# Exchanging halves of the rows by DMA in place of halves of the weights by VectorE

## The chip, the cores and the metric

One NeuronCore of a Trainium2 chip runs the kernel. The metric is the device time of one execution in microseconds (us), the median of several executions. Three executions of the kernel before took 1431.30, 1432.51 and 1433.72 us: the median is 1432.51 us.

## The reference

The input x has 8 sequences of 3584 tokens with 192 channels, 28672 rows in all.

1. A causal convolution over 7 tokens, whose 8 heads of 24 channels have softmaxed taps of their own, gives the rows.
2. Each row is normalised and multiplied with 8 normalised expert embeddings; the largest logit picks the expert, and the softmax of the logits at that place is the gate.
3. The row goes through the picked expert alone: `out = gate * (relu(row @ w1[e]) @ w2[e])`, with w1[e] 192 x 1024 and w2[e] 1024 x 192.

All is float32. The kernel carries nearly that precision through float16 matrices: each operand is a high half plus a low half, and a product is three float16 products (high x high, high x low, low x high).

## The kernel before

The rows are cut into 16 chunks of 1792 rows. For each chunk the kernel runs `mix` (convolution on TensorE, copies and squares on ScalarE and VectorE), then `route` (split into halves, transposition, logits, expert and position of each row), and then writes the chunk's rows to a table in DRAM (`rows_d`) that has one region for each expert, by 16 indirect DMAs from GpSimd. Each row of the table has the 192 high halves, then the low halves in the order of channels 128 to 191 and 0 to 127, then the token's number and its gate.

After chunks 2, 3, 4, 6, 9 and 12 and at the end (`PICK`, `hand_out`), blocks of 1024, 512 or 256 rows of one expert that are complete are appended to a list; blocks of 128 come at the very end. A block of 1024 is two entries of 512. Each entry is called a sub-block here; there are 92 sub-blocks in 88 blocks, numbered from 0. In the profile a sub-block has forty matmuls of line 750 and one transposing load of line 709, so that both can be counted off.

For a sub-block `expert` does this:

- `fetch` loads and transposes its rows from the table to SBUF by a transposing DMA (line 709, tile `e_xT`, three buffers), and its token numbers and gates by a small DMA (line 712). At the start of sub-block n, `fetch` is called for sub-block n+2. Where the list ends earlier, the call comes later. `e_xT` has three planes of 128 partitions: plane 0 the high halves of channels 0 to 127, plane 1 the high halves of channels 128 to 191 (partitions 0 to 63) and their low halves (64 to 127), plane 2 the low halves of channels 0 to 127.
- `copy_w1` and `copy_w2`, once for each block: VectorE copies the expert's image from `res` (all eight experts, in SBUF) to `slot`, since matmuls read at fixed addresses. The image has, side by side, W1's high part, W1's low part, one plane with the high (partitions 0 to 63) and low part (64 to 127) of W1's rows 128 to 191, and W2. `copy_w1` copies the first three (line 688, 3072 columns) and makes a fourth plane, the third with its halves exchanged, by two copies of 64 partitions (lines 690 and 691). It is called when the layer 1 of the sub-block before is written down, `copy_w2` (line 694) inside layer 1.
- Layer 1: each of eight groups of 128 hidden units takes five matmuls (line 750): plane 0 and plane 2 with W1's high part, plane 0 with W1's low part, plane 1 with the third plane of weights, plane 1 with the fourth. The last two give high x high plus low x low, and high x low plus low x high, of channels 128 to 191. The groups lie in PSUM tiles of 512 columns, for which a ring of five is shared with layer 2. ScalarE writes the rectified high half to `hid` (line 754), VectorE the low half (line 756).
- Layer 2: 24 matmuls for each 128 rows (line 773), scaled by the gate on ScalarE (line 778) and written to `out` by an indirect DMA from GpSimd (line 780).

SyncE's instructions, and with them all its DMAs, stand in the order in which the program writes them: the fetches, the transpositions of the routed rows (`turn`, line 580) and the loads of x (line 358) share this one queue, and one that waits holds all behind it. On the other engines a planner orders the instructions by a simulated time line, before the kernel runs; `under` and `behind` pin an instruction behind another of the same engine. `expert` is a generator: between its steps `run` writes down so many steps of `mix` and `route` as `steer` allots by fixed costs.

Before all that, `prep_load` and `prep_weights` bring each expert's weights to a staging area (in `hid`, `slot` or the end of `res`, in turn), measure their scale and split them into the image.

Of the kernel before, what the change touches and what calls it, by code (L numbers as in the profile page):

```python
# [37 lines left out]
RES = WS + 2  # L38
S2 = 4 * F
PAD = 128  # L40
# [15 lines left out]
LAND_X, LAND_T = 9.0, 4.5  # L56
TURN, FETCH, PIECE = 5.1, 2.1, 1.4
RANK_L, RANK_P = 2.0, 1.5
# [17 lines left out]
class _Moe:  # L76
    def __init__(self, ctx, tc, x, weight, emb, tau, w1, w2, out):
# [34 lines left out]
        self.weights_in, self.later = False, []  # L112
        self.subs, self.ready, self.at, self.copied = [], 0, 0, 0

# [151 lines left out]
    def prep_load(self, e):  # L266
        nc = self.nc


        st = (self.hid[:], self.slot[:], self.res[:, (E - 2) * RES:])[e % 3].bitcast(F32)[:, 0:2 * F + NFC * D]  # L270
        w1, w2 = self.w1[e], self.w2[e]
        nc.sync.dma_start(out=st[:, 0:F], in_=w1[0:128, :])
        nc.sync.dma_start(out=st[0:64, F:2 * F], in_=w1[128:192, :])
        nc.sync.dma_start(
            out=st[:, 2 * F:].rearrange("p (c d) -> p c d", d=D),
            in_=w2.rearrange("(c p) d -> p c d", p=128))
        return st

    def prep_weights(self, e, st):
# [3 lines left out]

        sr = st.bitcast(BF16).rearrange("p (n k) -> p n k", k=2)[:, :, 1]
        acc = self.sp.tile([128, 2], F32, tag="w_acc", name="w_acc")
        for k, cols in enumerate(
                ([(128, i) for i in range(NFC)] + [(64, i) for i in range(NFC, 2 * NFC)],
                 [(128, i) for i in range(2 * NFC, 2 * NFC + NFC * D // 128)])):
            if k and e >= BEHIND:

                i = nc.scalar.activation(
                    out=img[:, W2:W2 + NFC * D], in_=st[:, 2 * F:], func=AF.Square,
                    accum_out=acc[:, k:k + 1]).ins
# [4 lines left out]
            for n, (rows, i) in enumerate(cols):  # L298
                v = sr[0:rows, i * 128:(i + 1) * 128]
# [17 lines left out]
        b = img[:, W2:WS].rearrange("p (c d) -> p c d", d=2 * D)  # L317
        s_b = st[:, 2 * F:].rearrange("p (c d) -> p c d", d=D)
        hi = [nc.scalar.activation(out=o, in_=i, func=AF.Copy, scale=m).ins
# [357 lines left out]
    def copy_w1(self, at):  # L677
# [9 lines left out]
        v = self.res[:, bass.ds(self.we, W2)]  # L687
        nc.vector.tensor_copy(out=self.slot[:, 0:W2], in_=v)  # L688
        v = self.res[:, bass.ds(self.we + 2 * F, F)]
        nc.vector.tensor_copy(out=self.slot[0:64, W2:S2], in_=v[64:128, :])  # L690
        nc.vector.tensor_copy(out=self.slot[64:128, W2:S2], in_=v[0:64, :])  # L691

    def copy_w2(self):
        self.nc.vector.tensor_copy(  # L694
            out=self.slot[:, S2:], in_=self.res[:, bass.ds(self.we + W2, RES - W2)])
# [28 lines left out]


    def slack(self, T):
        pe = 5 * T / 2400
        return max(0, pe - (120 + T) / 960), max(0, pe - (172 + T) / 1200)


    def expert(self):
        nc, tc = self.nc, self.tc
        while self.ready < min(self.at + 3, len(self.subs)):
            self.fetch()
        u, xT, mt, T = self.subs[self.at][3:]
# [4 lines left out]
        w2 = self.slot[:, S2:S2 + WS - W2].rearrange("p (c d) -> p c d", d=2 * D)  # L740
        hh, hl = (self.hid[:, i * NFC * T:(i + 1) * NFC * T].rearrange(
# [3 lines left out]
        for b in range(0, NFC, m):  # L745
            ps = self.ps("h", [128, m, T], F32, "h_ps")
            for c in range(m):
                for i, (o, k) in enumerate(
                        ((0, 0), (0, 2), (F, 0), (2 * F, 1), (3 * F, 1))):
                    self.mm = nc.tensor.matmul(  # L750
                        out=ps[:, c, :], lhsT=w1(o, b + c), rhs=xT[:, k, :],
                        start=(i == 0), stop=(i == 4)).ins
# [13 lines left out]
            out=g[:, 0:nj], in0=mt[:, :, 1].bitcast(F32),  # L766
            scalar1=self.slot[:, S2 + WS - W2:S2 + WS - W2 + 2].bitcast(F32), scalar2=None, op0=ALU.mult)
        for a in range(nj):
# [193 lines left out]
```

## Time and profile before

| | |
|---|---|
| median of three executions | 1432.51 us |
| the profiled execution | 1439.81 us |
| its span, first to last instruction | 1438.1 us |
| TensorE busy in the span | 1199.9 us (83%) |
| VectorE busy | 862.3 us (60%) |
| ScalarE busy | 573.1 us (40%) |
| GpSimd busy | 547.5 us (38%) |
| mean granted TensorE clock | 0.913 of full speed |

The engines are PE (TensorE matmul), PEld (its weight loads, which overlap PE), DVE (VectorE), ACT (ScalarE), POOL (GpSimd) and SP (SyncE); a q behind the name is the engine's sequencer, which waits and issues DMAs. L750 is line 750 of the kernel before. A timeline row gives the start, the length, the engine, the line, what is written and what is read, the count of instructions merged in the row, and in brackets the idle time before it and what ended it.

### The profile page before, as it was taken

Reading aid. Unit: us, or ns where it says so; the run is one execution under the profiler, and the core shown is the slowest. Engines: PE = TensorE matmul, PEld = TensorE weight load, DVE = VectorE, ACT = ScalarE, POOL = GpSimd, SP = SyncE. Lnnn points to the kernel's source line nnn. Section 1 sums busy time; section 2 is a strip of 40 time slices with the busy share of each in tenths; the row PEclk is TensorE's granted clock in tenths of the full one; section 3 lists DMA queues with packets and bytes.
Section 4 is the critical chain, followed back from the end, with each engine's and each line's share of the span. In section 5 each row is a group of like instructions: output and inputs, shape, how many; then the busy total and the mean of one; then the engine's idle time right before and its main releaser. Section 6 shows DMA issues by size and latency. Waiting matters only on the chain. (4 is left out here: it accounts for less than half of the span.)

```text
span 1438.1 us, 28996 instructions
## 1 busy us (share of the span) xinstructions
PE 1199.9 (83%) x10560; PEld 918.6 (64%) x10560; DVE 862.3 (60%) x2208; ACT 573.1 (40%) x1345; POOL 547.5 (38%) x566
## 2 busy tenths in 40 slices
PE   5531956978878988899888989868999999999997
PEld 3421645856766756776554656636777676788797
DVE  3935666765866647677665666544454656467465
ACT  4734624344425425355335433222333333333332
POOL 0054042344454355445564455454222222222232
PEclk9655878988999989899999999979999999999999
DMA  8325262544445353573654452422121212012120
GB/s 249 116 71 177 55 148 53 114 111 113 101 116 119 83 137 82 123 135 79 142 142 96 104 118 73 93 68 65 44 48 40 46 41 57 28 42 60 32 49 22
DMA packets 273952, 129.11 MB, mean 90 GB/s; under 512 B 215774, under 2 KB 264285, under 8 KB 273808
## 3 DMA queue, kind: packets, MB, share of 16 engines
q1 hardware_dynamic: 250000, 80.39, 25.9%
q0 software_dynamic: 23808, 46.87, 11.0%
q8 instruction: 82, 1.34, 0.4%
q14 instruction: 62, 0.51, 0.1%
HBM read 38.35 MB, written 47.53 MB: 60 GB/s over the span
## 5 line engine op out<-in xcount | busy, mean ns | idle before, releaser
L750 PE MATMUL h_ps<-e_xT,slot 128*128 128x256 f16 (+2 forms) x3680 | 567.2, 307 | 48.1 <-issue 22.8
L773 PE MATMUL o_ps<-slot,hid 128*128 128x192 f16 x5544 | 523.2, 252 | 59.1 <-issue 18.7
L773 PEld LDWEIGHTS <-hid 128*128 128x128 f16 x5544 | 474.4, 100 | 107.1 <-issue 49.6
L780 POOL DMA_INDIRECT out_dram<-y,e_mt x231 | 261.5, 1132 | 586.3 <-ACT y L778 546.1
L750 PEld LDWEIGHTS <-slot 128*128 128x128 f16 x3680 | 330.0, 100 | 240.5 <-issue 76.3
L756 DVE SCALAR_TENSOR_TENSOR hid<-h_ps,hid 128x512 f16<-128x512 f32 x462 | 313.2, 687 | 203.4 <-ACT hid L754 178.1
L754 ACT ACTIVATE hid<-h_ps 128x512 f16<-128x512 f32 x462 | 267.7, 598 | 359.2 <-PE h_ps L750 236.2
L584 POOL DMA_INDIRECT rows_d<-rows,di x256 | 263.6, 1030 | 212.3 <-ACT hid L754 72.0
L778 ACT ACTIVATE y<-o_ps,g 128x192 f32<-128x192 f32 x231 | 91.6, 418 | 301.1 <-PE o_ps L773 165.7
L694 DVE COPY slot<-res 128x3074 f16 x88 | 85.8, 975 | 202.7 <-PE h_ps L750 150.9
L399 PE MATMUL conv_ps<-xt,band 128*112 128x384 f32 x256 | 108.7, 528 | 34.4 <-DMA xt<-in_dram 16.4
L404 ACT COPY xt<-conv_ps 112x384 f32<-112x384 f32 x128 | 60.3, 481 | 79.4 <-PE conv_ps L399 60.0
L688 DVE COPY slot<-res 128x3072 f16 x88 | 84.8, 963 | 9.2 <-remote 7.3
L485 PEld LDWEIGHTS <-xT 128*112 128x112 f16 x768 | 59.7, 145 | 37.2 <-DMA xT<-rows 17.0
L485 PE MATMUL lg_ps<-ma,xT 128*112 128x16 f16 x512 | 60.2, 201 | 20.4 <-DMA xT<-rows 12.0
L399 PEld LDWEIGHTS conv_ps<-xt,band 128*112 128x112 f32 x256 | 41.7, 189 | 52.0 <-issue 20.5
L411 ACT ACTIVATE sq<-xt 112x192 f32<-112x192 f32 x192 | 67.9, 357 | 3.9 <-DVE sq L414 2.8
L448 ACT CAST rows<-xt 112x768 f16<-112x768 f32 x64 | 49.9, 832 | 35.9 <-POOL rows L440 31.6
L446 DVE TENSOR_TENSOR xt<-xt,x_p_s 112x768 f32<-112x768 f32 x64 | 58.3, 948 | 0.0
L450 DVE TENSOR_TENSOR rows<-xt,rows 112x512 f16<-112x512 f32 x64 | 43.8, 684 | 15.7 <-ACT rows L448 15.6
L485 PE MATMUL lg_ps<-mb,xT 128*112 128x16 f16 x256 | 47.4, 204 | 1.5 <-ACT xT L481 1.5
L414 DVE SCALAR_TENSOR_TENSOR sq<-xt 112x192 f32<-112x192 f32 x64 | 22.6, 355 | 36.1 <-ACT sq L411 33.7
(165 smaller groups left out, 547.6 us busy)
## 6 DMA issues: line engine op xcount, KB each, us to landing
xt<-in_dram SPq DMA_DIRECT2D x39, 384.0 KB
xt<-in_dram SPq DMA_DIRECT2D x3, 1440.0 KB
rows_d<-rows,di POOLq DMA_INDIRECT x256
out_dram<-y,e_mt POOLq DMA_INDIRECT x231
xT<-rows SPq DMA_TRANSPOSE x224
xt<-in_dram SPq DMA_DIRECT2D x2, 1536.0 KB
hid<-in_dram SPq DMA_DIRECT2D x3, 768.0 KB
slot<-in_dram SPq DMA_DIRECT2D x3, 768.0 KB
```

The lines of the kernel that those rows point to most:

```text
L399: i = nc.tensor.matmul(out=ps, lhsT=self.band[:, h, :], rhs=xt[:, :, h * G:(h + 1) * G], start=True, stop=True).ins
L411: nc.scalar.activation(out=sq, in_=xc[:, t, :], func=AF.Square, accum_out=n2[:, t:t + 1])
L485: i = nc.tensor.matmul(out=lg[:, g * GX + a, :], lhsT=xT[:, a, k, :], rhs=self.mb if k == 1 else self.ma, start=(k == 0), stop=(k == 2)).ins
L584: i = self.nc.gpsimd.indirect_dma_start(out=self.rows_d[:, :], out_offset=bass.IndirectOffsetOnAxis(ap=idx, axis=0), in_=src, in_offset=No ...
L688: nc.vector.tensor_copy(out=self.slot[:, 0:W2], in_=v)
L694: self.nc.vector.tensor_copy(out=self.slot[:, S2:], in_=self.res[:, bass.ds(self.we + W2, RES - W2)])
L750: self.mm = nc.tensor.matmul(out=ps[:, c, :], lhsT=w1(o, b + c), rhs=xT[:, k, :], start=(i == 0), stop=(i == 4)).ins
L754: self.step = nc.scalar.activation(out=hh[:, b:b + m, :], in_=ps, func=AF.Relu).ins
L756: self.low = nc.vector.scalar_tensor_tensor(out=hl[:, b:b + m, :], in0=ps, scalar=0.0, in1=hh[:, b:b + m, :], op0=ALU.max, op1=ALU.subtrac ...
L773: self.mm = nc.tensor.matmul(out=o, lhsT=h[:, c, q], rhs=w2[:, c, k:k + D], start=(c + i == 0), stop=(c == NFC - 1 and i == 2)).ins
L778: self.step = nc.scalar.activation(out=y, in_=o, func=AF.Copy, scale=g[:, a:a + 1]).ins
L780: i = nc.gpsimd.indirect_dma_start(out=self.out[:, :], out_offset=bass.IndirectOffsetOnAxis(ap=mt[:, a, 0:1], axis=0), in_=y, in_offset=No ...
```

## The change

1. `copy_w1` no longer makes the fourth plane of weights; lines 690 and 691 go, and `slot` is 1024 columns shorter.
2. For each sub-block a new step `flip` makes a fourth plane of rows, `xf`: plane 1 with its halves exchanged, by two DMAs inside SBUF of 64 partitions each, from SyncE's queue, in two buffers. `flip` for sub-block n is written down ahead of `fetch` for sub-block n+1, and where that has not come by then, at the start of sub-block n.
3. The fifth matmul of a group takes the third plane of weights with `xf`; the others are as they were.
4. The one copy of W1 that stays is pinned behind the last low half written down (`under`).
5. The staging areas are dealt out anew, since `slot` is too short for one: W1 of experts 0, 3 and 6 goes to `slot` and their W2 to a stretch of `res` that the image of expert 7 takes later; experts 1, 4 and 7 use `hid`; 2 and 5 use the end of `res` as before.

```diff
-TURN, FETCH, PIECE = 5.1, 2.1, 1.4
+TURN, FETCH, PIECE, FLIP = 5.1, 2.1, 1.4, 0.9
...
+        self.fp = pool("flip", 2)
...
-        self.slot = self.cp.tile([128, S2 + RES - W2], F16, name="slot")
+        self.slot = self.cp.tile([128, RES], F16, name="slot")
...
-        st = (self.hid[:], self.slot[:], self.res[:, (E - 2) * RES:])[e % 3].bitcast(F32)[:, 0:2 * F + NFC * D]
+        tail = self.res[:, (E - 2) * RES:]
+        n1, n2 = 4 * F, 2 * NFC * D
+        s1, s2 = ((self.slot[:, 0:n1], tail[:, n1 + n2:n1 + 2 * n2]),
+                  (self.hid[:, 0:n1], self.hid[:, n1:n1 + n2]),
+                  (tail[:, 0:n1], tail[:, n1:n1 + n2]))[e % 3]
+        s1, s2 = s1.bitcast(F32), s2.bitcast(F32)
...
         v = self.res[:, bass.ds(self.we, W2)]
-        nc.vector.tensor_copy(out=self.slot[:, 0:W2], in_=v)
-        v = self.res[:, bass.ds(self.we + 2 * F, F)]
-        nc.vector.tensor_copy(out=self.slot[0:64, W2:S2], in_=v[64:128, :])
-        nc.vector.tensor_copy(out=self.slot[64:128, W2:S2], in_=v[0:64, :])
+        self.under(nc.vector.tensor_copy(out=self.slot[:, 0:W2], in_=v).ins)
...
     def fetch(self):
         nc, tc = self.nc, self.tc
+        if self.ready > self.flips:
+            self.flip()
...
+    def flip(self):
+        nc = self.nc
+        xT, mt, T = self.subs[self.flips][4:7]
+        xf = self.fp.tile([128, 512], F16, tag="xf", name="e_xf")[:, 0:T]
+        nc.sync.dma_start(out=xf[0:64, :], in_=xT[64:128, 1, :])
+        nc.sync.dma_start(out=xf[64:128, :], in_=xT[0:64, 1, :])
+        self.queue(FLIP)
+        self.subs[self.flips] = self.subs[self.flips][:4] + (xT, mt, T, xf)
+        self.flips += 1
...
         while self.ready < min(self.at + 3, len(self.subs)):
             self.fetch()
-        u, xT, mt, T = self.subs[self.at][3:]
+        if self.flips == self.at:
+            self.flip()
+        u, xT, mt, T, xf = self.subs[self.at][3:]
         self.copy_w1(self.at)
         self.at += 1
...
+        xk = [xT[:, 0, :], xT[:, 1, :], xT[:, 2, :], xf]
...
-                        ((0, 0), (0, 2), (F, 0), (2 * F, 1), (3 * F, 1))):
+                        ((0, 0), (0, 2), (F, 0), (2 * F, 1), (2 * F, 3))):
                     self.mm = nc.tensor.matmul(
-                        out=ps[:, c, :], lhsT=w1(o, b + c), rhs=xT[:, k, :],
+                        out=ps[:, c, :], lhsT=w1(o, b + c), rhs=xk[k],
```

## Rows read from the trace of the kernel before

**Rows 1.** stretch, length; busy us of PE, PEld, DVE, ACT, POOL; clock, DMA
```profile
...
160.00:950.00 790.00, 669.61 (x5581) 500.96 (x5580) 504.59 (x1450) 326.06 (x848) 373.19 (x381) 0.92 0.46 107
...
1100.00:1400.00 300.00, 288.20 (x2962) 234.87 (x2961) 176.44 (x291) 103.08 (x203) 76.84 (x68) 1.00 0.20 45
...
```

**Rows 2.** waits of TensorE from 160 to 950: total us, times, longest
```profile
...
PE h_ps L750 <- DMA e_xT<-rows_d: 10.0, 1, 10.0
PE o_ps L773 <- DVE hid L756: 8.8, 17, 2.0
...
PE o_ps L773 <- DVE slot L694: 3.7, 3, 1.8
...
```

**Rows 3.** waits of TensorE from 1100 to 1400, same columns
```profile
...
PE o_ps L773 <- DVE slot L694: 5.8, 13, 0.9
PE o_ps L773 <- DVE hid L756: 4.9, 11, 0.5
...
```

**Rows 4.** VectorE copies, groups by form: busy us, mean ns, idle before
```profile
...
L688 DVE COPY slot<-res 128x3072 f16 x88 | 84.8, 963 | 9.2 <-remote 7.3 <-PE h_ps L750 0.8 <-PE conv_ps L399 0.7
...
L691 DVE COPY slot<-res 64x1024 f16 x88 | 39.2, 446 | 1.5
L690 DVE COPY slot<-res 64x1024 f16 x88 | 37.4, 424 | 2.2
...
```

**Rows 5.** VectorE timeline around 609: start us, us, what
```profile
...
608.67 0.96 DVE L688 COPY slot<-res 128x3072 f16 x1
...
610.55 0.69 DVE L756 SCALAR_TENSOR_TENSOR hid<-h_ps,hid 128x512 f16<-128x512 f32 x1
...
```

**Rows 6.** ScalarE and VectorE timeline, preparation of weights
```profile
...
118.49 1.48 ACT L291 ACTIVATE res<-slot 128x1536 f16<-128x1536 f32 x1 [6.23 <-DMA slot<-in_dram]
...
129.08 1.81 DVE L323 SCALAR_TENSOR_TENSOR res<-hid,w_p_s,res 128x1536 f16<-128x1536 f32 x1
...
```

**Rows 7.** DMA issues on SyncE, 140 to 300: start us, us, what
```profile
...
147.73 1.28 SPq L709 DMA_TRANSPOSE e_xT<-rows_d  x1
...
179.46 23.22 SPq L580 DMA_TRANSPOSE xT<-rows  x16
...
204.08 1.28 SPq L709 DMA_TRANSPOSE e_xT<-rows_d  x1
...
```

**Rows 8.** TensorE timeline of line 750, same stretch
```profile
...
170.72 0.60 PE L750 MATMUL h_ps<-e_xT,slot 128*128 128x256 f16 x4
...
208.72 3.62 PE L750 MATMUL h_ps<-e_xT,slot 128*128 128x256 f16 x20 [10.03 <-DMA e_xT<-rows_d]
...
```

**Rows 9.** TensorE and SyncE timeline around sub-block 6
```profile
...
253.44 1.14 SPq L358 DMA_DIRECT2D xt<-in_dram  x2
...
253.94 1.80 PE L750 MATMUL h_ps<-e_xT,slot 128*128 128x256 f16 x15
...
255.60 1.25 SPq L709 DMA_TRANSPOSE e_xT<-rows_d  x1
...
```

**Rows 10.** TensorE and SyncE timeline around sub-block 38
```profile
...
781.30 0.52 PE L750 MATMUL h_ps<-e_xT,slot 128*128 128x512 f16 x1 [0.54 <-issue]
...
791.95 1.19 SPq L358 DMA_DIRECT2D xt<-in_dram  x2
...
792.88 3.40 PE L750 MATMUL h_ps<-e_xT,slot 128*128 128x512 f16 x15 [2.34 <-DVE xt L446]
...
794.15 2.19 SPq L709 DMA_TRANSPOSE e_xT<-rows_d  x1
...
796.56 0.41 SPq L712 DMA_DIRECT2D e_mt<-rows_d  x1
...
```

**Rows 11.** chain of waits, 880 to 890: a transposition lands
```profile
...
885.92 2.36 DMA xT<-rows
...
```

**Rows 12.** waits of SyncE over the whole span
```profile
...
SPq L709 <- PE h_ps L750: 325.8, 50, 14.1
SPq L580 <- DVE rows L453: 180.9, 12, 23.8
...
```

More of the change, by code (lines that the diff above doesn't have):

```diff
@@ L38 @@
 RES = WS + 2
-S2 = 4 * F
 PAD = 128
@@ L112, in __init__ @@
         self.weights_in, self.later = False, []
-        self.subs, self.ready, self.at, self.copied = [], 0, 0, 0
+        self.subs, self.ready, self.flips, self.at, self.copied = [], 0, 0, 0, 0
     def ps(self, ring, shape, dt, name):
@@ L267, in prep_load @@
         nc = self.nc
-        st = (self.hid[:], self.slot[:], self.res[:, (E - 2) * RES:])[e % 3].bitcast(F32)[:, 0:2 * F + NFC * D]
+        tail = self.res[:, (E - 2) * RES:]
[4 more added lines that the diff above has]
+        s1, s2 = s1.bitcast(F32), s2.bitcast(F32)
         w1, w2 = self.w1[e], self.w2[e]
-        nc.sync.dma_start(out=st[:, 0:F], in_=w1[0:128, :])
-        nc.sync.dma_start(out=st[0:64, F:2 * F], in_=w1[128:192, :])
+        nc.sync.dma_start(out=s1[:, 0:F], in_=w1[0:128, :])
+        nc.sync.dma_start(out=s1[0:64, F:2 * F], in_=w1[128:192, :])
         nc.sync.dma_start(
-            out=st[:, 2 * F:].rearrange("p (c d) -> p c d", d=D),
+            out=s2.rearrange("p (c d) -> p c d", d=D),
             in_=w2.rearrange("(c p) d -> p c d", p=128))
-        return st
+        return s1, s2
     def prep_weights(self, e, st):
@@ L281, in prep_weights @@
         img = self.res[:, e * RES:(e + 1) * RES]
-        sr = st.bitcast(BF16).rearrange("p (n k) -> p n k", k=2)[:, :, 1]
+        st, sw = st
+        sr, sv = (v.bitcast(BF16).rearrange("p (n k) -> p n k", k=2)[:, :, 1]
+                  for v in (st, sw))
         acc = self.sp.tile([128, 2], F32, tag="w_acc", name="w_acc")
         for k, cols in enumerate(
-                ([(128, i) for i in range(NFC)] + [(64, i) for i in range(NFC, 2 * NFC)],
-                 [(128, i) for i in range(2 * NFC, 2 * NFC + NFC * D // 128)])):
+                ([(sr, 128, i) for i in range(NFC)]
+                 + [(sr, 64, i) for i in range(NFC, 2 * NFC)],
+                 [(sv, 128, i) for i in range(NFC * D // 128)])):
             if k and e >= BEHIND:
                 i = nc.scalar.activation(
-                    out=img[:, W2:W2 + NFC * D], in_=st[:, 2 * F:], func=AF.Square,
+                    out=img[:, W2:W2 + NFC * D], in_=sw, func=AF.Square,
                     accum_out=acc[:, k:k + 1]).ins
@@ L297, in prep_weights @@
             tr = self.ps("h", [128, 128], F32, "tr_ps")
-            for n, (rows, i) in enumerate(cols):
-                v = sr[0:rows, i * 128:(i + 1) * 128]
+            for n, (v, rows, i) in enumerate(cols):
+                v = v[0:rows, i * 128:(i + 1) * 128]
                 i = nc.tensor.matmul(out=tr, lhsT=v, rhs=v, start=(n == 0),
@@ L687, in copy_w1 @@
         v = self.res[:, bass.ds(self.we, W2)]
[L688 to L691 removed]
+        self.under(nc.vector.tensor_copy(out=self.slot[:, 0:W2], in_=v).ins)
     def copy_w2(self):
         self.nc.vector.tensor_copy(
[L695 removed]
+            out=self.slot[:, W2:], in_=self.res[:, bass.ds(self.we + W2, RES - W2)])
     def fetch(self):
         nc, tc = self.nc, self.tc
+        if self.ready > self.flips:
+            self.flip()
         sel, j, n, u, need = self.subs[self.ready]
@@ L766, in expert @@
             out=g[:, 0:nj], in0=mt[:, :, 1].bitcast(F32),
-            scalar1=self.slot[:, S2 + WS - W2:S2 + WS - W2 + 2].bitcast(F32), scalar2=None, op0=ALU.mult)
+            scalar1=self.slot[:, WS:RES].bitcast(F32), scalar2=None, op0=ALU.mult)
         for a in range(nj):
```

4 lines of the change are left out of this document (2 added, 2 removed).

## The prediction

> **What bounds the kernel now.** I read the busy time by stretch first. From 160 to 950 us, where mixing, routing and experts run together, TensorE is busy 669.6 of 790 us; from 1100 to 1400, where only experts are left, 288.2 of 300 [rows 1]. So TensorE is the bound, and a change pays only through its idle time: 120 us in the middle, 12 us in the tail. VectorE is busy 504.6 of the 790 us, so it is not the bound, but it answers late. The second view is TensorE's waits, which say who ended that idle time: in the middle the low half of the hidden rows (line 756) 8.8 us and the copy of W2 (line 694) 3.7 us, and one wait of 10.0 us for a fetched sub-block [rows 2]; in the tail the same two engines' steps, 5.8 and 4.9 us [rows 3]. The third view is SyncE's queue against TensorE's time line, since the change adds to that queue.
>
> **Copies removed.** Lines 690 and 691 run 88 times each, 37.4 and 39.2 us [rows 4]: 76.6 us of VectorE, 0.87 us for each block. None of it is TensorE's own, so its worth is bounded by the waits on VectorE. Above: all of rows 2 and 3, 8.8 + 3.7 + 5.8 + 4.9 = 23.2 us. Below: nothing.
>
> **The copy of W1 behind the last low half.** In the row at 608.67 the three copies stand ahead of a low half, which starts at 610.55: 1.88 us late where VectorE was otherwise free for it [rows 5]. After the change this low half goes first, 0.69 us, and the copy, 0.96 us, ends 1.65 us after the point at which it used to start. The next layer 1 needs line 688's copy for its first matmul, which before was there after 0.96 us and now after 1.65; for its fifth matmul it needed the exchanged plane after 1.86 us. So the first matmul may start up to 0.69 us later and the fifth 0.21 us earlier. Behind a layer 2 of 512 or 256 rows this is covered; behind one of 128 rows it may not be. What goes is the late low half of rows 2 and 3, what can come is the later copy, both on the same waits. I take half of the 23.2 us for both edits together, 12 us; the ends are 23 and, should the pinned copy cost what the earlier low half gives, 0.
>
> **The two DMAs for each sub-block: issue.** A small issue of SyncE takes 0.41 us at 796.56 and 0.60 at 791.95 (1.19 for two) [rows 10]; I take the nearest, two of 0.41, 0.82 us, 75 us over 92 sub-blocks. SyncE waits far longer than that, 325.8 us for the buffers of fetches and 180.9 us for rows to be transposed [rows 12], so I cost the issue itself at nothing; where it runs transpositions back to back, each `flip` moves what follows by 0.82 us. The added waits, for the fetched rows to land and for a buffer, hold the fetches and transpositions behind them; the buffer comes free with the same layer 1 that the next fetch waits for anyway.
>
> **The landing.** No plain transfer inside SBUF is in the trace. The nearest is a transposition from SBUF to SBUF: it lands 2.36 us after its issue ends [rows 11]. The other end is a fetch from DRAM: issue over at 205.36, TensorE goes on at 208.72 [rows 7, 8], 3.36 us. I take 2.36.
> The Trainium skill speaks against two DMAs of 64 partitions each: "SBUF — State Buffer", section "Can I just issue two DMAs to hit both halves?", says that two such transfers on the two halves serialise. By its 196 GB/s for 64 partitions the second would add, as an estimate, 0.33 us for 64 KB; ten bare sub-blocks (below) would cost 3 us more, and the sum would end at 1445. No row here shows it.
>
> **The landing, where nothing hides it.** This is the term that decides. `flip` for sub-block n stands right ahead of `fetch` n+1, about 1.0 us before that fetch starts (793.14 to 794.15, [rows 10]), so its data are there 0.82 + 2.36 − 1.0 = 2.2 us after the old start of fetch n+1. Before the change, layer 1 of n needed only fetch n. I laid the 92 starts of line 709 beside the 92 starts of layer 1. From sub-block 46 on fetch n+1 starts 6.9 us or more ahead of layer 1 of n, so all is hidden there. In the middle ten sub-blocks have less than 2.2 us: 2, 3, 6, 13, 14, 18, 21, 27, 32 and 38.
> - Sub-block 2: fetch 3 starts at 204.08, behind 16 transpositions that take SyncE 23.2 us [rows 7]. Layer 1 of sub-block 2 began at 170.72 [rows 8]; it can now end only after 206.3. In that stretch TensorE had nothing better, so its work moves behind 206: forty matmuls of 256 columns at half of 0.227 us (3.40/15, [rows 10]) and layer 2's 48 at 192/512 of it, 4.5 + 4.1 = 8.6 us.
> - Sub-block 6, the pattern of eight: layer 1 starts at 253.94, the queue is free at 254.58, the data land at 257.8 [rows 9]: 3.8 us. The others are 0.5, 3.8, 1.0, 2.2, 3.6, 3.7 and 4.8 us; with it 23.4 us.
> - Sub-block 38: layer 1 runs from 781.30 to 796.3; the queue is free at 793.14, the data land at 796.3 [rows 10]. The stall is 15 us long, but TensorE loses no more than the layer's forty matmuls, 9.1 us.
> - Sub-block 0: its `flip` waits for its own fetch, so the transfer is bare: 0.82 + 2.36 less four matmuls, some 2.5 us.
>
> Together 43.6 us. Two things soften it: the first four matmuls of a group don't read `xf`, and with five PSUM tiles the planner may put up to four groups' first sixteen ahead (16 x 0.227 = 3.6 us), if its own time line shows the delay; and a stall is partly paid back from the 120 us of later idle time. Against nothing and 43.6 I take half, 22 us.
>
> **Staging.** Expert 7's square (1.48 us) at 118.49 waited 6.23 us for its load; now it must wait for expert 6's split of W2, which ended at 130.89 [rows 6], while expert 6's own square need no longer stand behind that load. From 6 us earlier to 3 us later (two squares); I take 0.
>
> **Sum.** 22 − 12 = 10 us more. Against the profiled execution's own 1439.81 us (span 1438.1) that is 1450; it ran 7.3 us over the median, so the median becomes 1432.5 + 10 = 1442.5.
>
> **The rivals.**
> - The freed VectorE wins: the planner sees the late transfers and fills them with the first four matmuls of each group, so only sub-blocks 2 and 38 cost, half of 17.7 us, 9, while all 23 us of waits go and preparation gains its 6. That is 9 − 23 − 6 = −20 at best; with two thirds of the gain, −10. Time 1413 to 1430, middle 1421. For it: the late low half of rows 5 recurs over the whole middle. Against it: only 12.5 us of the middle's 120 are ended by those two. It decides if the ten stalls together stay below about 12 us.
> - The queue loses in full: all 43.6 us, and 8 us of gain: 1468. For it: SyncE stands behind transpositions in nine of the ten places, and those now start later too. Against: idle time to pay with.
> - Neither shows: the stalls fall into idle time that other causes keep (107 of the middle's 120 us have other causes than those of rows 2 that are VectorE's), and the copies were hidden. For it: in the tail, where half of the copies stand, only 12 us are idle at all. Against it: sub-block 2, whose work has no other place. Time 1432.5, give or take 3.
>
> **How the numbers follow.** A measurement of this kernel tells 0.2%, 2.9 us, from no change. Forecast (1436 to 1455) 0.43, freed VectorE 0.31, full loss 0.14, neither 0.12. Faster: the first rival, 0.31. Same: neither, and a tenth left over, 0.12. Slower: 0.57. The two larger cases have different signs, so the range runs from 1419 to 1466; the forecast's own is 1436 to 1455.
>
> **What would show it.** Right: in the waits of TensorE after, line 750 waits for a DMA that writes `e_xf`, at sub-blocks 0, 2, 38 and at the last sub-block before each hand-out, 15 to 30 us in all; SyncE shows two issues of about 0.4 us ahead of each line 709; VectorE's busy time is 70 to 77 us lower; no low half starts behind a copy of W1. Wrong: the waits on `e_xf` are under 10 us, or the idle time of TensorE from 160 to 950 falls below 120 us; or the tail (from 1100 on) changes by more than 10 us, for which only the pinned copy could be the reason.

## The result, and the profile after

The changed kernel takes 1415.52 us (median of 4 runs, 1414.44 to 1418.61), the kernel before 1431.90 (1428.97 to 1433.72) on the same chip: ratio 0.9886, 95% interval [0.9857, 0.9915]. That is 16 us faster; 10 us slower was forecast, and the time lies 3.5 us under the range. The profiled run took 1418.61 us (span 1416.9). Executions that ran at a lower granted clock throughout are left out of all medians below: there was one, 1533.48 us at 0.80 of full speed, in the run with ScalarE's queue.

In other series of runs the sign is the other one. Two of them, in which the kernel before takes 1315 and 1317 us, gave 1.0147 [1.0117, 1.0177] and 1.0139 [1.0110, 1.0168]: 18 to 20 us slower. So two results have to be explained. Below, "the first kind" are series of runs in which the kernel before takes 1429 to 1432 us, as in the profile ahead of the prediction, "the second kind" those in which it takes 1314 to 1317. All runs of one series are of one kind. That the chip decides the kind is not shown: the chip's number noted with the runs is 15 for a series at 1316.67 us and again, eight minutes later, for one at 1431.02, and whether it was the same chip is not known. It is not the program: in the profiles of the changed kernel on both kinds TensorE, ScalarE, GpSimd and SyncE run the same instructions in the same order, and VectorE all but a few of 2032.

First the busy times of the changed kernel on the first kind: the page's row (busy us, share of the span), then the two stretches of [rows 1].

```profile
PE 1192.6 (84%) x10560; PEld 913.3 (64%) x10560; DVE 802.8 (57%) x2032; ACT 587.3 (41%) x1345; POOL 548.7 (39%) x566
```

```profile
160.00:950.00 790.00, 664.36 (x5610) 501.69 (x5609) 475.51 (x1388) 328.60 (x842) 378.06 (x385) 0.92 0.49 113
...
1100.00:1400.00 300.00, 293.41 (x3034) 238.51 (x3032) 163.56 (x239) 110.89 (x207) 75.78 (x69) 1.00 0.25 52
```

VectorE is busy 59.5 us less, not 76.6. The two copies' time is gone in full (without their rows the kernel before would have had 785.9 us busy), but the rows that are left overlap each other less than before: the low halves, each as long as before, fill 9 us more. TensorE's idle time in the middle grew from 120.4 to 125.6 us, in the tail it fell from 11.8 to 6.6. TensorE's waits, from 160 to 950 and then from 1100 to 1400 (total us, times, longest):

```profile
PE o_ps L794 <- issue: 23.8, 31, 1.9
PE h_ps L771 <- DMA e_xf<-e_xT: 18.0, 6, 7.0
PE h_ps L771 <- issue: 17.6, 12, 9.3
PE pc_ps L544 <- DVE rc L541: 10.2, 4, 4.2
...
PE o_ps L794 <- DVE hid L777: 7.1, 6, 2.5
PE h_ps L771 <- DVE hid L777: 6.5, 2, 5.7
```

```profile
PE o_ps L794 <- ACT hid L775: 2.4, 3, 0.8
PE o_ps L794 <- DVE hid L777: 2.2, 7, 0.4
```

Against [rows 2, 3]: the waits for the W2 copy are gone (3.7 and 5.8 us), the low half's wait in the tail is 2.2 for 4.9, and waits on `e_xf` are new. In the middle the waits for low halves have not become less: 7.1 and 6.5 us, before 8.8 and 1.6.

Sub-block 2 behaves as the prediction drew it. SyncE's DMA issues (start us, us):

```profile
170.71 22.22 SPq L588 DMA_TRANSPOSE xT<-rows  x16
...
193.60 0.52 SPq L737 DMA_DIRECT2D e_xf<-e_xT  x1
194.17 0.61 SPq L738 DMA_DIRECT2D e_xf<-e_xT  x1
195.50 1.28 SPq L716 DMA_TRANSPOSE e_xT<-rows_d  x1
```

TensorE at line 771, the same stretch:

```profile
167.50 1.47 PE L771 MATMUL h_ps<-e_xT,slot 128*128 128x256 f16 x12
168.94 0.60 PE L771 MATMUL h_ps<-e_xT,slot 128*128 128x256 f16 x4
...
198.48 0.39 PE L771 MATMUL h_ps<-e_xf,slot 128*128 128x256 f16 x1 [9.32 <-issue]
```

Sixteen matmuls that don't read `e_xf` run ahead, four for each of four groups; the first that reads it starts at 198.48, 3.7 us after the issue. The wait is put down to "issue", so it is missing from the 18.0 us above; with it they are 27.3. Yet nothing of it is left soon after: sub-block 9 starts at 271.8 us here and at 273.9 in the same kernel without exchanges (below; on the second kind at 254.9 and 250.6, but there sub-block 0 is already 3.6 us apart). The expensive place is sub-block 20, which the prediction did not list.

### The profile page after: what moved, and what is told of

Read it like the earlier page. It is cut to its first block, busy times and chain, and to the rows that moved or that the text cites. A ratio compares the mean times of both kernels' runs of the same rounds, so it can differ in the third digit from the quotient of the medians.

```text
span 1416.9 us, 28937 instructions
## 1 busy us (share of the span) xinstructions
PE 1192.6 (84%) x10560; PEld 913.3 (64%) x10560; DVE 802.8 (57%) x2032; ACT 587.3 (41%) x1345; POOL 548.7 (39%) x566
## 2 busy tenths in 40 slices
DMA packets 288672, 136.70 MB, mean 96 GB/s; under 512 B 221406, under 2 KB 279005, under 8 KB 288528
## 5 line engine op out<-in xcount | busy, mean ns | idle before, releaser
L794 PE MATMUL o_ps<-slot,hid 128*128 128x192 f16 x5544 | 515.2, 251 | 47.8 <-issue 27.8
L771 PE MATMUL h_ps<-e_xT,slot 128*128 128x256 f16 (+2 forms) x2944 | 513.5, 307 | 27.4 <-ACT y L799 7.7
L794 PEld LDWEIGHTS <-hid 128*128 128x128 f16 x5544 | 469.7, 100 | 91.8 <-issue 43.7
L771 PE MATMUL h_ps<-e_xf,slot 128*128 128x256 f16 (+2 forms) x736 | 221.7, 307 | 29.0 <-DMA e_xf<-e_xT 18.0
L799 ACT ACTIVATE y<-o_ps,g 128x192 f32<-128x192 f32 x231 | 94.8, 419 | 358.7 <-PE o_ps L794 278.6
L407 PE MATMUL conv_ps<-xt,band 128*112 128x384 f32 x256 | 108.9, 529 | 26.0 <-DMA xt<-in_dram 18.2
```

The source lines that it names most:

```text
L407: i = nc.tensor.matmul(out=ps, lhsT=self.band[:, h, :], rhs=xt[:, :, h * G:(h + 1) * G], start=True, stop=True).ins
L771: self.mm = nc.tensor.matmul(out=ps[:, c, :], lhsT=w1(o, b + c), rhs=xk[k], start=(i == 0), stop=(i == 4)).ins
L794: self.mm = nc.tensor.matmul(out=o, lhsT=h[:, c, q], rhs=w2[:, c, k:k + D], start=(c + i == 0), stop=(c == NFC - 1 and i == 2)).ins
L799: self.step = nc.scalar.activation(out=y, in_=o, func=AF.Copy, scale=g[:, a:a + 1]).ins
```

## The experiments

Starts of layer 1 in us, by sub-block (the last column is the end of the last layer 2); each line is one profiled run, those of the second kind from two series:

| kind, kernel | 0 | 9 | 18 | 21 | 46 | end |
|---|---|---|---|---|---|---|
| first: before | 147.5 | 289.6 | 416.6 | 457.8 | 964.9 | 1432.2 |
| first: after | 140.6 | 271.8 | 398.7 | 453.3 | 951.9 | 1411.0 |
| first: without exchanges | 139.1 | 273.9 | 395.0 | 428.1 | 917.5 | 1375.3 |
| second: before, staging new | 127.4 | 253.8 | 361.7 | 405.0 | 846.9 | 1303.7 |
| second: after | 129.6 | 254.9 | 362.7 | 422.6 | 881.6 | 1330.2 |
| second: without exchanges | 126.0 | 250.6 | 355.4 | 390.3 | 831.3 | 1283.3 |

**The change in parts, second kind** (the kernel before 1313.75 us). The expectations of these four runs were written with times of the first kind in mind; the runs are of the second, so only differences can be held against them. First the kernel before with the new staging areas alone, everything else as it was:

```diff
-        st = (self.hid[:], self.slot[:], self.res[:, (E - 2) * RES:])[e % 3].bitcast(F32)[:, 0:2 * F + NFC * D]
+        s1, s2 = ((self.slot[:, 0:n1], tail[:, n1 + n2:n1 + 2 * n2]),
+                  (self.hid[:, 0:n1], self.hid[:, n1:n1 + n2]),
+                  (tail[:, 0:n1], tail[:, n1:n1 + n2]))[e % 3]
```

> The kernel before with the new staging areas alone (slot keeps its length, the copies of lines 690 and 691 stay, no flips). Theory A, the gains come in three separate places (preparation about 6.5 us, middle about 2 to 8, tail about 6.5): the first layer 1 starts 6 to 7 us earlier and the time falls by 4 to 7 us, to 1425 to 1428. Theory B, the early start is given back where TensorE later waits for chunks, and all of the gain is the freed VectorE: first layer 1 equally early, but a time within 2 us of before.

Measured: 1313.61 us, ratio 0.9992 [0.9962, 1.0022]. Staging alone is worth nothing there, and the earlier start that both theories name is missing too: layer 1 starts at 127.4 us, with the old staging (in the run without the two copies, below) at 127.7. Then the changed kernel with its copy of W1 unpinned:

```diff
-        self.under(nc.vector.tensor_copy(out=self.slot[:, 0:W2], in_=v).ins)
+        nc.vector.tensor_copy(out=self.slot[:, 0:W2], in_=v)
```

> The changed kernel without the pin of the W1 copy behind the last low half. Theory A1, the shorter copies make the tail faster: time within 2 us of the changed kernel, some 1414 to 1417, and TensorE's waits on VectorE's low halves and W2 copy from 1100 on stay below 5 us. Theory A2, the order of the low half ahead of the copy makes the tail faster: the tail from sub-block 47 on is 4 to 7 us longer again, time 1419 to 1423.

Measured: 1341.09, ratio 1.0193 [1.0157, 1.0229]. Against the changed kernel's 1334.85 in another series of this kind the pin is worth some 6 us, as theory A2 has it, though the intervals of the two ratios overlap. Next, VectorE's time given back to it as four dead copies for each block (352 copies, 78.8 us), pinned like the copy of W1:

```diff
+        for k in range(4):
+            p, q = ((0, 64), (64, 0))[k % 2]
+            v = self.res[:, bass.ds(self.we + 2 * F + 256 * k, 256)]
+            self.under(nc.vector.tensor_copy(out=self.dead[p:p + 64, :], in_=v[q:q + 64, :]).ins)
```

> The changed kernel with VectorE work put back: for each block four dead copies of 64 x 256 from the other half of the partitions, about 0.9 us, behind the W1 copy (their output is not read). Theory A1, VectorE's freed time is worth 6 to 12 us: 1421 to 1428. Theory A2, freed time is worth nothing by itself, only order and staging count: within 2 us of the changed kernel, 1414 to 1418.

Measured: 1341.01, ratio 1.0191 [1.0155, 1.0226]: some 6 us over the changed kernel for 79 us of VectorE, the low end of theory A1 (the intervals of the ratios overlap here too). Its time by itself is cheap, at least where TensorE waits for exchanges anyway; the same copies in the kernel without exchanges were not run. Last, the changed kernel without exchanges:

```diff
-        xf = self.fp.tile([128, 512], F16, tag="xf", name="e_xf")[:, 0:T]
-        nc.sync.dma_start(out=xf[0:64, :], in_=xT[64:128, 1, :])
-        nc.sync.dma_start(out=xf[64:128, :], in_=xT[0:64, 1, :])
-        self.queue(FLIP)
+        xf = xT[:, 1, :]
```

> The changed kernel without the flips: the fifth matmul reads plane 1 as it is, so the exchange of channels 128 to 191 is left out of the computation, and SyncE issues no DMA for it. What the flips cost in the changed kernel is the difference. Theory A, the waits for e_xf that show (18.0 us in the middle, 9 us more at sub-block 2) are mostly paid back from other idle time: faster by 0 to 8 us, 1407 to 1415. Theory C, they are lost in full: faster by 18 to 27 us, 1388 to 1398.

Measured: 1290.85, ratio 0.9817 [0.9780, 0.9855]: 23 us under the kernel before, and 44 under the changed kernel (next), more than either theory has.

**The changed kernel itself, and earlier exchanges** (the kernel before 1314.60 us). No edit:

> The changed kernel once more, beside the kernel before on whatever chip these runs get. Theory A (the chip decides): the exchanged halves cost TensorE about 50 us of waits everywhere, and what is won (about 23 us without those waits, by the run without exchanges, 1290.9 against 1313.8) is not enough where TensorE has no waits on instructions of its own to pay with. So where the kernel before takes about 1314 us this takes 1335 to 1346 (ratio 1.015 to 1.025), and where the kernel before takes about 1432 us it takes 1410 to 1422 (ratio 0.985 to 0.993). Theory B (the pin decides): the unpinned version lost 1.9% only because its copies of W1 stand ahead of the low halves; then this kernel is at 0.98 to 0.995 of before on both kinds of chip.

Measured: 1334.85, ratio 1.0147, just under theory A's 1335 to 1346. Theory B is out: the change loses on this kind, and the exchanges cost 44 us (1334.85 less 1290.85; 43.7 within one series, below). More than half of the 44 arise at sub-block 20 (table: from 18 to 21 the changed kernel takes 59.9 us, without exchanges 34.9). SyncE and TensorE of the changed kernel there, second kind:

```profile
379.79 0.42 SPq L719 DMA_DIRECT2D e_mt<-rows_d  x1
393.40 10.66 SPq L588 DMA_TRANSPOSE xT<-rows  x8
404.12 0.59 SPq L737 DMA_DIRECT2D e_xf<-e_xT  x1
404.75 0.59 SPq L738 DMA_DIRECT2D e_xf<-e_xT  x1
```

```profile
389.79 1.47 PE L771 MATMUL h_ps<-e_xT,slot 128*128 128x256 f16 x12
394.77 0.60 PE L771 MATMUL h_ps<-e_xT,slot 128*128 128x256 f16 x4 [3.50 <-ACT y L799]
399.57 0.17 PE L544 MATMUL pc_ps<-rc,lth 112*128 112x8 f16 x1 [4.21 <-DVE rc L541]
...
406.66 0.40 PE L771 MATMUL h_ps<-e_xf,slot 128*128 128x256 f16 x1 [6.89 <-DMA e_xf<-e_xT]
```

The exchange of sub-block 20 stands behind eight transpositions, and these wait until 393.4 for VectorE to write their rows. TensorE has nothing else to do: of the three waits only the last is put down to `e_xf`, but all three lie within this layer 1. The granted clock falls in the pause. Three stretches of 10 us of the changed kernel (length, busy PE, PEld, DVE, ACT, POOL, then the granted clock), second kind:

```profile
390.00:400.00 10.00, 2.06 (x18) 1.47 (x15) 7.38 (x22) 3.86 (x7) 4.62 (x4) 0.77 0.21 47
400.00:410.00 10.00, 3.34 (x12) 2.01 (x13) 1.89 (x6) 1.08 (x2) 0.94 (x1) 0.50 0.46 98
410.00:420.00 10.00, 10.00 (x79) 7.47 (x76) 2.94 (x4) 4.60 (x9) 2.80 (x3) 0.88 0.66 137
```

and first kind, at the same sub-block:

```profile
423.00:433.00 10.00, 2.43 (x22) 1.83 (x20) 8.60 (x27) 3.86 (x7) 4.55 (x4) 0.76 0.28 64
433.00:443.00 10.00, 4.36 (x21) 2.95 (x22) 0.87 (x2) 1.66 (x3) 0.93 (x1) 0.56 0.40 82
```

TensorE stands idle 14.6 and 13.2 of 20 us, and in the second ten the granted clock is 0.50 and 0.56: all or most of what it does there runs at the lower of its two levels, 1.2 GHz. Two kernels try to undo the late exchanges. In the first the exchange of sub-block 2 goes right behind the first three fetches, and a hand-out's last exchange goes as soon as the list is at its end:

```diff
-        if self.flips == self.at:
+        if self.ready == len(self.subs) and self.flips < self.ready:
             self.flip()
...
         while self.ready < min(3, len(self.subs)):
             self.fetch()
+        if self.ready > self.flips:
+            self.flip()
```

> The changed kernel with the exchange of sub-block 2 issued right behind the first three fetches, and, where a hand-out's list has come to its end, the exchange of its last sub-block issued as soon as that is fetched and not with the next fetch. Theory A (late exchanges are the loss): the waits of TensorE on e_xf fall below 10 us from 160 to 950, sub-block 2 ends its layer 2 near 167 to 175 us rather than 195, and the time is 1290 to 1315 where the kernel before takes 1314 (ratio 0.98 to 1.00), or 1385 to 1410 where it takes 1432. Rival C (the waiting exchanges hold up SyncE's queue, wherever they stand): the exchange now stands earlier in the queue and holds transpositions behind it, so the time stays within 0.5% of the changed kernel's.

Measured: 1330.71, ratio 1.0123 [1.0093, 1.0153], 4 us under the changed kernel. TensorE's waits from 160 to 950:

```profile
PE h_ps L771 <- DMA e_xf<-e_xT: 25.3, 8, 6.8
PE lg_ps L493 <- DMA xT<-rows: 19.8, 26, 2.2
PE h_ps L771 <- DMA e_xT<-rows_d: 13.4, 2, 11.0
```

Sub-block 20 now ends layer 2 at 400.6 us instead of 421.6, and 21 starts 17.9 us earlier (404.9 against 422.8, the changed kernel in the same series). But at 46 only 8 are left (873.4 against 881.4): the issues of the exchanges of 25 and 28 end 4.5 and 5.0 us after their layer 1 starts (0.1 and 3.9 in the changed kernel), and two fetches are waited for, 13.4 us. Rival C's figure comes true (within 0.5% of the changed kernel) and theory A's don't (25.3 us of waits on `e_xf`, not under 10). Yet the place costs, as A said; a stall mended in SyncE's order comes back at the next one. The second has only the exchange of sub-block 2 early (the last two lines of the diff):

> The changed kernel with one edit: the exchange of sub-block 2 stands behind the first three fetches, ahead of the sixteen transpositions, and all others stay where they are. If sub-block 2 alone displaced some 28 us of work (its layer 2 ended at 195 against 167 us), as theory A in its strong form has it, this kernel is 15 to 28 us under the changed kernel of the same chip. If its work was made up for elsewhere, it is within 4 us of it, and the loss lies with the other late exchanges, which the kernel with all of them earlier then shows.

Measured: 1339.47, ratio 1.0187 [1.0155, 1.0219], 4.6 us over the changed kernel; layer 2 of sub-block 2 ends at 167.4 us instead of 195.3, and at 46 nothing of it is left (881.3 against 881.4). The 28 us stall of sub-block 2 is made up elsewhere. Then, the kernel before without the two copies; its fifth matmul reads the third plane of W1 as the fourth does:

```diff
-        v = self.res[:, bass.ds(self.we + 2 * F, F)]
-        nc.vector.tensor_copy(out=self.slot[0:64, W2:S2], in_=v[64:128, :])
-        nc.vector.tensor_copy(out=self.slot[64:128, W2:S2], in_=v[0:64, :])
...
-                        ((0, 0), (0, 2), (F, 0), (2 * F, 1), (3 * F, 1))):
+                        ((0, 0), (0, 2), (F, 0), (2 * F, 1), (2 * F, 1))):
```

> The kernel before with only the two copies of exchanged halves of W1 taken out; its fifth matmul reads the third plane of W1 as the fourth does, so the exchange is left out. No transfers are added, the copy of W1 stays where it was. If the copies removed are what the change gains: 1286 to 1296 us where the kernel before takes 1314 (as the changed kernel without exchanges, 1290.9), ratio 0.978 to 0.986. If the pinned copy of W1 is what gains: within 0.4% of the kernel before. Where the kernel before takes 1432 us: 1395 to 1412 by the first, 1427 to 1437 by the second.

Measured: 1293.46, ratio 0.9840 [0.9811, 0.9870]: 21 us of the 23 to 26 that the change gains without its exchanges are the two copies. Since 79 us of dead copies behind the last low half cost 6, this points to the copies' place, ahead of low halves and of the layer 1 that waits for them, rather than to their length. It is not shown: those dead copies ran in a kernel that waits for exchanges.

**Stalls that the planner doesn't know of.** ScalarE and VectorE of the kernel before have long waits for which the profile finds no releaser ("remote", "issue"). Three ScalarE rows, first kind, before:

```profile
ACT hid L754 <- remote: 70.0, 14, 12.7
...
ACT y L778 <- issue: 29.1, 8, 5.2
...
ACT hid L754 <- issue: 27.7, 14, 14.7
```

and second kind, the changed kernel:

```profile
ACT y L799 <- issue: 6.7, 4, 3.2
...
ACT hid L775 <- issue: 2.3, 2, 1.7
```

Summed over all rows of TensorE, ScalarE and VectorE they are 267 us on the first kind (before; 335 after, 268 without exchanges) and 21 on the second (before with the new staging). The "remote" ones can be traced to TensorE. In the kernel before all 26 of them, 131 us, are waits for the semaphore that only TensorE's instructions raise, and its update comes over 1.5 us after the last of these has ended by the profile. One such place of the changed kernel, first kind, with TensorE's last row ahead of it:

```profile
923.87 0.38 PE L771 MATMUL h_ps<-e_xf,slot 128*128 128x512 f16 x1
...
929.42 0.97 DVE L699 COPY slot<-res 128x3074 f16 x1 [10.28 <-remote]
...
929.47 0.42 ACT L799 ACTIVATE y<-o_ps,g 128x192 f32<-128x192 f32 x1 [11.82 <-remote]
```

The update comes at 929.39. Such stretches, from the end of the matmul to the late update, fill 90 us before, 88 after and 77 without exchanges on the first kind, and none on the second (a last one of 6.8 us, at the very end, which every run has, is not counted). The kinds lie 117, 81 and 91 us apart in the same three kernels. The sizes suggest that most of this distance is TensorE finishing later than its rows say; no run takes these stretches away, and what holds TensorE up in them is not shown. To see what such waits do to the change, dead work was put into the finished order of both kernels: ahead of the first relu of 22 sub-blocks (3 to 45, every second) thirty one-column activations, ahead of the first low half of 11 of them one reduction of 5120 elements. The core of it:

```diff
+    for k, (step, low) in enumerate(MARKS[3:46:2]):
+        for name, n in ((step, 30), (low, 1 if k % 2 == 0 else 0)):
...
+                at = next(p for p, v in enumerate(body) if v.name == name)
+                body.insert(at, i)
```

Their groups in the kernel before (busy us, mean ns, idle before):

```profile
L962 ACT ACTIVATE dead<-dead 128x1 f16<-128x1 f16 x660 | 66.1, 194 | 8.7 <-issue 8.7
...
L965 DVE TENSOR_REDUCE dead<-dead 128x1 f16<-128x5120 f16 x11 | 60.3, 5478 | 0.0
```

In a series of the first kind (the kernel before 1429.23 us):

> The kernel before with stalls that the planner doesn't know of: ahead of the first relu of every second sub-block from 3 to 45 (22 places) ScalarE runs thirty dead one-column activations, and ahead of the first low half of every fourth (11 places) VectorE one dead reduction of 5120 elements, put into the finished order. They stand for the waits of ScalarE and VectorE on nothing that the profile shows, which the kernel before has where it takes 1432 us (145 and 72 us in all) and has not where it takes 1314. Both theories: about 22 x 5.7 us of ScalarE and 11 x 5.3 us of VectorE, of which TensorE sees a part; 1350 to 1430 us. It is the base for the next two.

> The changed kernel with the same stalls at the same sub-blocks. Theory A (late exchanges hide behind waits that TensorE has anyway; with few such waits they cost in full): it is between 20 us below and 5 us above the kernel before with the same stalls, against 20 us above it without them. Rival D (the gain on the one chip comes from where that chip's own waits happened to fall, and has nothing to do with how many there are): it stays 14 to 25 us above the kernel before with stalls.

> The changed kernel without exchanges (the fifth matmul reads plane 1 as it is) and with the same stalls: it tells how much of the 44 us, by which the exchanges cost TensorE without stalls (1334.9 against 1290.9), is left among them. Theory A: 0 to 25 us under the changed kernel with stalls. Rival D: 38 to 50 us under it.

Measured: 1473.15 for the kernel before with stalls, 1443.47 for the changed kernel, 1435.15 for the changed kernel without exchanges. With stalls the change gains 30 us instead of 16, and the exchanges cost 8. The 30 us lie outside theory A's range for the difference (20 us under to 5 over); its direction holds, and rival D is out. In a series of the second kind (the kernel before 1316.67 us), with the changed kernel and the one without exchanges beside them:

> The changed kernel as it is, as the base for the next. Where the kernel before takes 1429 to 1432 us: 1410 to 1420; where it takes 1314: 1330 to 1340.

> The changed kernel without exchanges, no stalls added. On a chip where the kernel before takes about 1430 us: if the late exchanges hide behind that chip's own waits, 0 to 15 us under the changed kernel (1400 to 1416), and the gain of the removed copies is what it was elsewhere, 20 to 30 us under the kernel before. If instead the exchanges cost their 44 us there too and the copies gain more: 1365 to 1378. On a chip where it takes 1314: 1286 to 1295, as before.

> The kernel before with the stalls of ScalarE and VectorE put into its finished order. Where the kernel before takes 1429: 1468 to 1478 again. Where it takes 1314: 1350 to 1375 (the 44 us that they cost on the other kind of chip, or a little more, since fewer waits are there to take them in).

> The changed kernel with the same stalls. Where the kernel before takes 1429: 25 to 35 us under the kernel before with stalls, again. Where it takes 1314: if waits of ScalarE and VectorE are what hides late exchanges, from 15 us under to 8 us above the kernel before with stalls, so at least 12 us better than without them (20 us above); if another property of the slower kind of chip does it, 14 to 25 us above.

Measured: 1334.84, 1291.11 (exchanges 43.7 us), 1358.34 and 1361.30. The change costs 18.2 us without stalls and 3.0 with them, the first of the two cases expected. So on both kinds the same stalls cost the kernel before 42 to 44 us and the changed kernel 26 to 28, and move the comparison by 13 to 15 us in the change's favour. How much of that is the exchanges' is known for the first kind alone; without exchanges and with stalls nothing was run on the second.

**Other ways for the exchange.** In the first of these two series (first kind) the two DMAs were given to ScalarE's queue, right behind each fetch:

```diff
-        nc.sync.dma_start(out=xf[0:64, :], in_=xT[64:128, 1, :])
-        nc.sync.dma_start(out=xf[64:128, :], in_=xT[0:64, 1, :])
+        nc.scalar.dma_start(out=xf[0:64, :], in_=xT[64:128, 1, :])
+        nc.scalar.dma_start(out=xf[64:128, :], in_=xT[0:64, 1, :])
```

> The changed kernel with both exchange DMAs issued by ScalarE's queue, right behind each fetch in the program and placed by the planner, in place of SyncE's queue one fetch later. If the loss is the exchanges' place in SyncE's queue, behind transpositions and buffers: TensorE's waits on e_xf below 10 us from 160 to 950, and 1290 to 1305 where the kernel before takes 1314 (1380 to 1405 where it takes 1432). If it is the transfer itself, or if ScalarE is held up by its waits for the fetched rows and by 184 more issues: 1320 to 1345, with waits on relu (line of the high half) in place of those on e_xf.

Measured: 1455.84, 27 us over the kernel before and 40 over the changed kernel. TensorE hardly waits for `e_xf` any more (1.0 us), but ScalarE stands before its relu:

```profile
ACT hid L771 <- remote: 81.8, 16, 26.5
...
ACT hid L771 <- issue: 67.5, 48, 2.8
```

The second row tells: in the kernel before it is 27.7 us, and of the 67.5 some 53 have the issue of an exchange inside them; the 184 issues take ScalarE's queue 107 us. The first row is little evidence, since the kernel before has 70.0 us of the same. So it is the second outcome of the expectation: the wait moved to the engine that TensorE needs most. Last, in another series of the first kind (the kernel before 1431.02), the exchanged halves straight from DRAM:

```diff
+        for p, c in ((0, D), (64, 128)):
+            lds.append(nc.sync.dma_start_transpose(
+                out=xf[p:p + 64, :],
+                in_=self.rows_d[:].bitcast(F16)[bass.ds(row, T), c:c + 64]).ins)
```

> The changed kernel with the exchanged halves fetched from DRAM: two transpositions of 64 columns each beside every fetch, into a third buffer (for which the output's tiles go from four to three), in place of the two transfers inside SBUF one fetch later. Nothing waits for fetched rows on SyncE any more. If place and wait are the loss: no waits on e_xf over 3 us, 1290 to 1310 where the kernel before takes 1314 to 1317 (1390 to 1412 where it takes 1430). If the two transpositions, estimated at 1.3 us of SyncE each from the 1.28 us of a fetch, 184 of them, 239 us, make SyncE's queue late instead: 1325 to 1360, with TensorE's waits on e_xT and on xT up by 20 us or more.

Measured: 5502.22 us, ratio 3.847. The page's row of DMA packets shows why (the changed kernel has 288672):

```profile
DMA packets 4061603, 136.72 MB, mean 25 GB/s; under 512 B 4003422, under 2 KB 4051933, under 8 KB 4061456
```

Fourteen times the packets for the same bytes: a transposition of 64 columns is taken apart into single elements (3784704 packets are of 2 bytes). Neither outcome of the expectation came. The Trainium skill, "DMA: Bandwidth & Descriptors", section "DMA Transpose (X-bar)", says that inputs from DRAM with fewer than 128 columns may fall back to a rearranged access pattern with inefficient descriptors; this trace agrees. The idea itself was not tested by it. And the changed kernel without exchanges, first kind, no stalls:

> The changed kernel without exchanges, once more. Where the kernel before takes about 1430 us: 1400 to 1416 if late exchanges hide behind that chip's own waits (0 to 15 us under the changed kernel's 1415), 1365 to 1378 if they cost their 44 us there too. Where it takes 1314 to 1317: 1288 to 1294 again.

Measured: 1381.90, ratio 0.9649 [0.9621, 0.9676], 49 us under the kernel before. The exchanges cost 34 us there (1415.5 less 1381.9), 10 less than on the second kind. The expectation's second case, 1365 to 1378, is nearer than its first: most of the late exchanges' cost does not hide there. What differs most is the other term: 49 us of gain against 23 to 26.

## Why the prediction was wrong

The sum was "22 − 12 = 10 us more". Both terms were halved, and both were larger:

| term, us | predicted | first kind | second kind |
|---|---|---|---|
| exchanges that come late | +22 (ends 0 and 43.6) | +34 | +44 |
| copies, pin and staging | −12 (ends −23 and 0; staging 6 earlier to 3 later) | −49 | −23 to −26 |
| sum | +10 | −16 | +18 to +20 |

- **The step that failed is the upper bound of the gain**: "its worth is bounded by the waits on VectorE. Above: all of rows 2 and 3". On the first kind, where the forecast was made and measured, the gain is 49 us, twice that bound. Those rows are two stretches, 23.2 us; over the whole span TensorE waited 61.8 us on VectorE. And the gain is not VectorE's alone. Between the kernel before and the changed one without exchanges, first kind, TensorE's waits, summed over their rows, fall from 230.1 to 186.7 us (on VectorE 61.8 to 39.1, on ScalarE 74.2 to 60.0, the rest 6.5) and its own busy time from 1199.9 to 1184.7 us, as the granted clock rises from 0.913 to 0.928. On the second kind the same comparison (new staging in both) gives 18.6 us of waits and 3.7 of busy time, and the gain, 23 to 26 us, is about the bound itself; there only the halving was wrong.
- **The exchanges' term was the right size before it was halved**: 43.6 us in full, 43.7 measured on the second kind. The agreement is partly luck, for the places differ. Of the ten sub-blocks listed, the second kind shows waits on `e_xf` at 2, 6, 18, 27 and 32, and besides at 15, 20, 25, 28 and 31; on the first kind 2 and 6, then 20, 25, 27, 28 and 31. Sub-block 2, charged with 8.6 us, costs nothing by sub-block 46, 38 has no such wait, and 20, which had fetch 21 3.1 us ahead and was therefore left out, makes 21 to 25 us of it. A lead read from the trace of before doesn't hold once each exchange has moved the queue.
- **"A stall is partly paid back from the 120 us of later idle time"** is not what happens on the first kind: of 44 us only 10 go. With stalls added, only 8 us of the exchanges are left, so it does happen where there are more waits of other kinds.
- **Staging, taken at 0**: on the first kind layer 1 starts 6.9 us earlier (8.4 without exchanges). Expert 6's square no longer stands behind the load [rows 6], and the first fetch is issued at 130.49 instead of 137.01:

```profile
113.29 1.48 ACT L299 ACTIVATE res<-res 128x1536 f16<-128x1536 f32 x1 [3.96 <-DVE res L331]
...
130.49 6.25 SPq L716 DMA_TRANSPOSE e_xT<-rows_d  x1
```

  That is the 6 us end of the range given, but not all of it belongs to this place: ScalarE's split of the expert ahead (105.68 us for 108.61) is already 2.9 us early, that of expert 6 (115.94 for 122.61) 6.7. On the second kind old and new staging start within 2 us of each other (127.7 against 126.0 to 129.6).
- **The landing**, taken as 2.36 us from the end of the issue: that row was misread. 885.92 [rows 11] is where an issue starts, which ends at 887.16, so the row counts from the start and leaves 1.1 us. On the first kind `e_xf` arrives 2.3 to 3.5 us after the second issue in five of six waits (1.3 in the sixth, at sub-block 20), three of them nearer to the other end (3.36). The issue was 0.82 for two and is 1.1 to 1.2.
- **What should have shown it**: two issues stand ahead of each fetch, 27.3 us of waits on `e_xf` lie in the 15 to 30 named, idle time in the middle stays over 120 us. No low half starts right behind a copy of W1 (66 did before). All of the signs named for "right" came, but for VectorE's 59.5 us and sub-blocks 0 and 38, which have no wait on `e_xf`, and the time went the other way: none of them measured the gain.

The rival "the freed VectorE wins" names the time (1413 to 1430), not the reason: it wanted the stalls below 12 us, and they are 34. Shown by runs: the sizes of both terms on both kinds, the two copies as the source of 21 us, sub-block 20 as the chief place, and that added waits on ScalarE and VectorE favour the change. Not shown: why the removed copies are worth twice as much on the first kind. Of the 23 to 26 us between the kinds some 7 are the earlier first layer 1. The added stalls don't explain the rest: they make the exchanges cheaper (34 to 8) but the other term smaller too (49 to 38), while between the kinds it is the other term that grows. TensorE's late updates, 90 us before and 77 without exchanges, may be a part of it, but profiles of this kind differ by more (77 to 107 us in seven). What makes TensorE late there stays open, and the new staging alone was not run on that kind.

## What to carry to other kernels

An engine's removed work is not bounded by the waits that end with it: here TensorE's waits on ScalarE fell too, and its own busy time, at a higher granted clock. A DMA that needs another DMA's data, put into an in-order queue, costs where that queue holds something late ahead of it; read which instruction stands before it at each hand-over, and don't count on the leads of the old trace. Where the gain and the loss are of one size, the sign can differ from one series of runs to the next, so measure in several, and on several chips, before deciding; none of the kernels with the two DMAs was faster than the kernel before on the second kind.

## What the runs showed of the hardware

- One program takes 1429 to 1432 us in some series of runs and 1314 to 1317 in others, some 9% apart, and each repeats to about 1%. The traces differ in waits without a releaser, 267 against 21 us on three engines. Those called "remote" wait for TensorE's semaphore, which comes late: 90 us of such stretches before, none on the second kind. Often ScalarE and VectorE are let go by it at the same moment: 929.4 and 929.5 us in the changed kernel, after 10.3 and 11.8 us.
- TensorE loses more than a stall's length: at sub-block 20 it was idle 13 to 15 of 20 us, and in the second ten of them the granted clock was 0.50 to 0.56; a matmul of 256 columns took 0.42 us there and 0.27 soon after (439.68 and 442.70 us, first kind).
- Two plain transfers of 64 partitions inside SBUF need 1.1 to 1.2 us of SyncE, and their reader went on 2.3 to 3.5 us after the second issue (1.3 once); 64-column transpositions from DRAM made the kernel 3.8 times as long.
